# A gated linear recurrence with a GEGLU layer behind it: group order by chunk instead of by batch, and the log-magnitude from summed squares

## The chip, the cores and the metric

The kernel runs on one core of a Trainium2 chip. The metric is the device time in microseconds (us), from the start of the program to its end. Before the change it is 317.31 us, the median of 13 runs (312.91 to 322.17).

## What is computed

Four batches, eight heads, 768 time steps, head dimension 48. The first half is a recurrence with a complex decay for each head and channel, whose real part alone is read out; its output, 3072 tokens of 384 channels, goes through a gated GELU layer with a residual:

```python
mag = sqrt(a_re**2 + a_im**2)
a = (a_re + 1j * a_im) * minimum(mag, 0.999) / (mag + 1e-6)
for t in range(768):                      # per batch and head
    S = a[t, :, None] * S + k[t, :, None] * v[t, None, :]
    y[t] = q[t] @ real(S)
x = y.transpose(0, 2, 1, 3).reshape(3072, 384)
g = x @ w_gate                            # 384 x 1536
h = 0.5 * g * (1 + erf(g / sqrt(2))) * (x @ w_val)
out = x + sigmoid(x @ w_res) * (h @ w_out)
```

## The kernel before

**Recurrence as masked attention.** The product of decays from one step to another is the exponential of a difference of cumulative sums. So the kernel takes the logarithm of each decay (log-magnitude `lm` and phase `th`), sums both along time by matmuls with triangular matrices, and multiplies q by the exponential of the sum (`E`) and its cosine and sine, k by the inverse exponential (`Ei`) and the same cosine and sine. Inside 128 tokens the recurrence then is a masked product of such q and k with v; what lies before is carried as a state of 96x48 per head (`G`, and its bf16 copy `Gb`).

**Groups, units, stages.** A group is one batch and one of its three chunks of 256 tokens, and within it two halves of 128 tokens, so there are 12 groups. In the program they are numbered batch by batch (`b, s = divmod(g, NS)` in `rows`): group 0, 1, 2 are the three chunks of batch 0. The number s of the chunk decides how a group begins: s = 0 with an empty state, s = 1 and 2 with what the chunk before left. Units hold the groups that go through the GELU layer together: [0], [1, 2], [3, 4], [5, 6], [7, 8], [9, 10], [11]. For each unit u there are two stages, which follow one another, X(u) then Y(u):

- X(u), `phase_x` (L550): the log and exp pass of the groups of unit u+2 (`p1_steps`, L189), the cumulative sums of log-magnitude of unit u+1 (`cs_l`, L216) and their exps, then arctans of unit u+2 (`p1_arctan`), the cumulative sums of the phase of unit u+1 (`cs_t`, L246) with the reduction of the angle to a fraction of a turn (two DVE operations per half, then one that clears the sign), the sines and cosines (`p2_sin`, L270), the second half of the attention of unit u, and the output products of unit u-1 (`op_step`, L501). X(-1) and X(0) differ: X(-1) does all of it for group 0 alone, and X(0) does the log pass and the sums for groups 1 and 2 and then the log pass for 3 and 4.
- Y(u), `phase_y` (L599): the gate and value products of unit u with their gelus (`gv_step`, L474: twelve sets of a PSUM tile `gp` and one `vp`, one gelu on ACT, one multiplication on DVE), the residual gate (`rp_step`, L491), the products of q and k with exps and sines of unit u+1 (`products`, L327) and the first half of the attention of unit u+1 (`attention`, L354).

The order inside a stage is written out by hand: `weave` places each list of steps between two fractions of the stage and emits the steps in that order; each engine works off its own queue in that order. Log and exp, arctan and sine, and gelu and tanh each need a table of ACT's; so a stage X has two table loads and a stage Y one (`table`, L517), 21 in all, and a manual dependence keeps every ACT function that needs a table in emitted order.

**The log pass of one group** takes, on 128x768 tiles, four ACT operations and three on DVE:

```python
lm = Ln(ar);  s = Exp(-lm);  th = s * ai;  s = Square(th)
s = Ln(s + 1);  lm = min(0.5 * s + lm, LNMAX)     # arctan(th) comes later
```

**The decay over a chunk border** is needed as a factor per head and channel (`M`) laid out along the partitions. For groups 1, 2 and 4 it comes from matmuls with a vector of ones (`sums`, 48 of them, and `sums_exp`). For later groups with s > 0, three rows (the first log-magnitude, the last `E` of the group before, the first `Ei`) are written to DRAM and read back transposed by POOL's DMA queue (`turn`, L279; `decay0` to `decay3`), and `decay3` multiplies them on DVE at the end of the X stage. For groups from `TURN` = 5 on, q and k are transposed by DMA (`trp`); before, by TensorE.

**Loads.** SP's queue issues, in this order, a of group 0 (real and imaginary part, each in two halves: L143 to L147), q and k of group 0 (L150), a of groups 1 to 4, q and k of 1 and 2, and later groups. POOL's queue holds v (L157), and the weights (L163): `after_landing` (L178) places a tiny POOL copy that reads a loaded tile, and issues the weights behind it; so weights come after a of groups 1 to 4 has landed, w_out after k of group 2. Tiles of a are in pools of six buffers (`lda`), q and k in pools of four (`ldq`); the products go to tiles of their own (`pK`). Outputs are written by SP (`ot`), and x is accumulated onto them in DRAM by POOL's queue (L514).

## Time and profile before

| what | value |
|---|---|
| median of 13 runs | 317.31 us (312.91 to 322.17) |
| the profiled execution, its own time | 316.8 us |
| its span, first to last instruction | 315.0 us |
| granted clock of TensorE, mean | 0.938 of full speed |
| TensorE matmuls (PE) | 261.2 us busy, 83% of the span |
| TensorE weight loads (PEld, beside PE) | 161.0 us, 51% |
| VectorE (DVE) | 226.2 us, 72% |
| ScalarE (ACT) | 194.3 us, 62% |
| GpSimd (POOL) | 81.1 us, 26% |
| DMA | 41.87 MB, mean 133 GB/s |

The stages, from the table load on ACT that begins each to the next stage's:

| stage | from | length, us | PE busy | DVE busy | ACT busy |
|---|---|---|---|---|---|
| loads and X(-1) | 0.00 | 23.50 | 5.86 | 8.12 | 10.22 |
| X(0) | 23.50 | 41.65 | 27.24 | 32.06 | 28.59 |
| Y(0) | 65.15 | 18.99 | 18.14 | 16.30 | 12.09 |
| X(1) | 84.14 | 18.67 | 13.47 | 13.85 | 17.20 |
| Y(1) | 102.81 | 25.47 | 25.05 | 22.36 | 16.69 |
| X(2) | 128.28 | 18.79 | 15.75 | 14.31 | 17.04 |
| Y(2) | 147.07 | 23.81 | 21.71 | 16.74 | 11.53 |

Busy time is the time in which an engine executes; an engine that waits for another's result is not busy. The row with the highest busy time in a stage is the engine that would set the stage's length if nothing else did; where no row comes near the length, the stage is a chain of waits. Line numbers (L134) are those of the kernel before; `act` and its L134 issue all ACT functions, so those are told apart by their tiles.

### The profile page before, as it was taken

To read this page: it belongs to the slowest core of one execution; us is meant where nothing else is said; L and a number is where in the kernel's file an instruction comes from. 1 tells how busy PE (TensorE), PEld (TensorE's weight loads), DVE (VectorE), ACT (ScalarE), POOL (GpSimd) and SP (SyncE) were. 2 spreads that over 40 slices of the span, in tenths; PEclk is the share of its full clock that TensorE was granted. 3 is DMA by queue.
4 is the path that set the end of the run, shared out by engine and by line. 5 is a ranking of instruction groups with operands and counts; after the bars stand their busy time and mean duration, and the time that the engine had idled before them with its cause. 6 is when DMAs were issued, how large, how long until landed. Compare 5 with 4: busy or idle time off the path is not lost.

```text
span 315.0 us, 5372 instructions
## 1 busy us (share of the span) xinstructions
PE 261.2 (83%) x1976; PEld 161.0 (51%) x1976; DVE 226.2 (72%) x404; ACT 194.3 (62%) x325; POOL 81.1 (26%) x119
## 2 busy tenths in 40 slices
PE   0336936879967999789979989999999996999994
PEld 0115633568734566445436654566545663446682
DVE  1346857879569997299944899887997767445452
ACT  4539686276798756997427976559664644355150
POOL 4105641013051502047202374101711031200220
PEclk9995675959999999999979999999999998999999
DMA  7999999999999995079997389930399014910531
GB/s 155 205 192 190 189 161 173 169 193 193 180 186 206 206 189 41 0 138 172 190 221 94 44 149 130 218 66 25 55 183 211 0 28 100 183 27 0 131 71 52
DMA packets 166874, 41.87 MB, mean 133 GB/s; under 512 B 155968, under 2 KB 166848, under 8 KB 166848
## 3 DMA queue, kind: packets, MB, share of 16 engines
q1 hardware_dynamic: 132416, 30.94, 51.2%
q0 software_dynamic: 34432, 10.59, 31.4%
q8 instruction: 15, 0.25, 0.3%
q14 instruction: 11, 0.09, 0.1%
HBM read 31.31 MB, written 9.07 MB: 128 GB/s over the span
## 4 chain that ended last, share of the span: by engine, by line
PE 59%; ACT 14%; DVE 10%; DMA 7%; issue 4%; SPq 4%; POOL 0%; DVEq 0%; ACTq 0%
PE gp L481 14%; PE vp L485 13%; PE op L505 9%; ACT s L134 4%; ACT L519 3%; PE cst L259 3%; PE rp L497 3%; PE csl L222 3%; DMA ar<-in_a_re_dram 3%; ACT ar L134 2%; SPq L146 2%; PE at L372 2%; DMA KT<-padK 2%; PE cst L261 2%; SPq L154 2%
## 5 line engine op out<-in xcount | busy, mean ns | idle before, releaser
L134 ACT ACTIVATE h<-gp 128x512 bf16<-128x512 f32 (+1 forms) x84 | 44.8, 536 | 47.1 <-PE gp L481 46.7
L481 PE MATMUL gp<-xT,wg 128*128 128x512 bf16 (+1 forms) x252 | 63.1, 355 | 2.1 <-DVE xT L472 1.1
L488 DVE SCALAR_TENSOR_TENSOR h<-h,vp 128x512 bf16<-128x512 bf16 (+1 forms) x84 | 50.2, 606 | 20.2 <-PE vp L485 16.5
L485 PE MATMUL vp<-xT,wv 128*128 128x512 bf16 (+1 forms) x252 | 63.3, 354 | 0.0
L505 PE MATMUL op<-wo,h 128*128 128x384 bf16 x288 | 52.5, 333 | 4.9 <-ACT Ei L134 3.0
L505 PEld LDWEIGHTS <-h 128*128 128x128 bf16 x288 | 28.1, 100 | 23.9 <-issue 8.2
L514 POOL DMA_DIRECT2D out_dram<-x x22 | 20.7, 954 | 66.3 <-DMA out_dram<-ot 62.3
L485 PEld LDWEIGHTS <-wv 128*128 128x128 bf16 x252 | 24.7, 100 | 21.2 <-issue 1.2
L481 PEld LDWEIGHTS <-wg 128*128 128x128 bf16 x252 | 23.9, 100 | 18.9 <-issue 2.9
L519 ACT ACT_TABLE_LOAD x21 | 26.9, 1283 | 1.1 <-PEq L657 0.7
L160 POOL DMA_DIRECT2D v<-in_v_dram x24 | 22.1, 924 | 4.5 <-issue 1.9
L375 DVE TENSOR_TENSOR atm<-at,mask 128x512 bf16<-128x512 f32 x28 | 19.2, 685 | 5.4 <-PE at L372 5.4
L199 DVE TENSOR_TENSOR ai<-s,ai 128x768 f32<-128x768 f32 x12 | 11.1, 955 | 16.4 <-ACT s L134 10.8
L259 PE MATMUL cst<-ai,lt0b 128*128 128x384 f32 x24 | 11.9, 579 | 12.9 <-ACT ai L134 11.0
L134 ACT ACTIVATE CS<-ai,hpi 128x768 bf16<-128x768 f32 x11 | 10.3, 933 | 17.9 <-DVE ai L267 17.9
L222 PE MATMUL csl<-ar,lt0a 128*128 128x384 f32 x24 | 11.5, 567 | 11.0 <-DMA ar<-in_a_re_dram 11.0
L508 DVE SCALAR_TENSOR_TENSOR ot<-sg,op 128x384 f32<-128x384 f32 x24 | 13.2, 548 | 9.6 <-PE op L505 8.4
L181 POOL COPY landed<-k 1x1 f32<-1x1 f32 x10 | 3.4, 338 | 63.6 <-DMA k<-in_k_dram 63.6
L438 ACT CAST x<-y 128x384 bf16<-128x384 f32 x24 | 11.5, 478 | 12.5 <-PE y L435 11.3
L286 POOL DMA_DIRECT2D m<-dm x20 | 16.9, 884 | 8.8 <-DMA dm<-Ei 4.5
L398 DVE TENSOR_TENSOR atm<-at,mask 128x512 bf16<-128x512 f32 x20 | 13.7, 686 | 5.1 <-PE at L395 5.0
L134 ACT ACTIVATE sg<-rp 128x384 f32<-128x384 f32 x24 | 11.7, 492 | 8.2 <-PE rp L497 8.2
(98 smaller groups left out, 513.7 us busy)
## 6 DMA issues: line engine op xcount, KB each, us to landing
ar<-in_a_re_dram SPq DMA_DIRECT2D x24, 192.0 KB, 5.0
ai<-in_a_im_dram SPq DMA_DIRECT2D x24, 192.0 KB, 4.7
q<-in_q_dram SPq DMA_DIRECT2D x24, 192.0 KB, 4.0
k<-in_k_dram SPq DMA_DIRECT2D x24, 192.0 KB, 4.0
out_dram<-ot SPq DMA_DIRECT2D x24, 192.0 KB, 2.6
out_dram<-x POOLq DMA_DIRECT2D x22, 192.0 KB, 4.3
v<-in_v_dram POOLq DMA_DIRECT2D x24, 96.0 KB, 5.4
wg<-in_moe_w_gate_dram POOLq DMA_DIRECT2D x4, 288.0 KB, 10.9
```

Source lines behind the costliest of these rows:

```text
L134: tab(nc.scalar.activation(**kw))
L160: nc.gpsimd.dma_start(out=t[:, c], in_=rows(v, g, c))
L222: nc.tensor.matmul(out=cs, lhsT=lmat[c], rhs=T["lm", g][:, sl], start=True, stop=True)
L259: nc.tensor.matmul(out=cs, lhsT=tmat[c], rhs=th[:, sl], start=True, stop=(s == 0))
L286: nc.gpsimd.dma_start(out=m[u * D:(u + 1) * D].rearrange("p r h -> p (r h)"), in_=md.rearrange("r (h d) -> d (r h)", h=H))
L375: nc.vector.tensor_tensor(out=atm, in0=at, in1=mask4, op=OP.mult)
L481: nc.tensor.matmul(out=gp, lhsT=wg[:, fi, ffi * 128:(ffi + 1) * 128], rhs=xT[:, fi, :], start=(fi == 0), stop=(fi == KD - 1))
L485: nc.tensor.matmul(out=vp, lhsT=wv[:, fi, ffi * 128:(ffi + 1) * 128], rhs=xT[:, fi, :], start=(fi == 0), stop=(fi == KD - 1))
L488: nc.vector.scalar_tensor_tensor(out=h2[:, ffi, :], in0=h2[:, ffi, :], scalar=0.5, in1=vp, op0=OP.mult, op1=OP.mult)
L505: nc.tensor.matmul(out=ps, lhsT=h2[:, ffi, jj * 128:(jj + 1) * 128], rhs=wo[:, ffi, :], start=(ffi == 0), stop=(ffi == KF - 1))
L514: nc.gpsimd.dma_start(out=out[t0:t0 + 128, :], in_=T["x", token(u, jj)], accum_op=OP.add)
L519: tab(nc.scalar.preload_act_table_set(nm))
```

## The change

- **Order.** Groups are numbered by chunk: the first chunk of all four batches is groups 0 to 3, the second 4 to 7, the third 8 to 11. What is carried (the phase sum `R`, the state `G`) is kept per batch. Units stay as they are.
- **Log-magnitude.** `lm` is half of Ln(ar*ar + ai*ai). The two Squares and the addition are emitted in Y stages (`squares`), tied behind the last gelu and the last gate multiplication emitted before; the log pass keeps Ln(lm), Ln(ar), Exp(-Ln(ar)), and one DVE operation takes the half and the minimum.
- **First stages.** `ramp` replaces X(-1) and X(0): groups 0, 1 and 2 share one log and exp pass and one pass of arctans and sines; 19 table loads in all. Group 0's attention is written out as a whole (`attention_first`). X(1) does the log pass and the sums of unit [3, 4] together; X(2) those of [5, 6] and the log pass of [7, 8] (`P1AT`); from X(3) on the log pass is again two units ahead.
- **Decays.** All eight groups with s > 0 take the way through DRAM; `sums` and `sums_exp` are gone; the multiplication is placed at 0.55 of Y.
- **Memory and loads.** q and k are multiplied in place; pools change sizes. Loads of weights and of q, k and a of groups 1 to 4 wait for the landing of a named earlier load (`held`); SP issues those of groups 1 to 4 behind three small row copies (`T["row"]`).

```diff
     UNITS = [[0]] + [[g, g + 1] for g in range(1, NG - 1, 2)] + [[NG - 1]]
     NU = len(UNITS)
-    FIRST = UNITS[0][-1]
-    NEAR = UNITS[2][-1]
+    ORD = [(b, s) for s in range(NS) for b in range(B)]
+    assert NS == 3 and B == 4 and len(ORD) == NG
+    CHUNK = [b * NS + s for b, s in ORD]
+    NEXT = {g: ORD.index((b, s + 1)) for g, (b, s) in enumerate(ORD) if s < NS - 1}
+    P1AT = {2: 1, 3: 2, 4: 2}
...
     lda = ctx.enter_context(tc.tile_pool(name="lda", bufs=6))
-    ldq = ctx.enter_context(tc.tile_pool(name="ldq", bufs=4))
+    ldr = ctx.enter_context(tc.tile_pool(name="ldr", bufs=4))
+    pB = ctx.enter_context(tc.tile_pool(name="pB", bufs=1))
+    ldq = ctx.enter_context(tc.tile_pool(name="ldq", bufs=3))
     ldv = ctx.enter_context(tc.tile_pool(name="ldv", bufs=6))
-    pS = ctx.enter_context(tc.tile_pool(name="pS", bufs=2))
+    pS = ctx.enter_context(tc.tile_pool(name="pS", bufs=4))
     pE = ctx.enter_context(tc.tile_pool(name="pE", bufs=2))
...
-    xp = ctx.enter_context(tc.tile_pool(name="xp", bufs=9))
+    xp = ctx.enter_context(tc.tile_pool(name="xp", bufs=8))
...
     def rows(a, g, c):
-        b, s = divmod(g, NS)
+        b, s = ORD[g]
         t0 = (s * C + c) * 128
...
+    def held(i, after):
+
+        if after is not None:
+            tc.add_manual_dep(i.ins, after.ins.name, behind, reason="load order")
+        return i
...
+    def squares(g):
+
+        def q0():
+            T["lm", g] = pS.tile([128, W], FP, tag="s", name="lm")
+            with paced("gelu"):
+                nc.scalar.activation(out=T["lm", g], in_=flat(T["ar", g]), func=AF.Square)
+
+        def q1():
+            t = pB.tile([128, W], FP, tag="sq", name="sq")
+            with paced("gelu"):
+                nc.scalar.activation(out=t, in_=flat(T["ai", g]), func=AF.Square)
+            with paced("gmul"):
+                nc.vector.tensor_tensor(out=T["lm", g], in0=T["lm", g], in1=t, op=OP.add)
+        return [q0, q1]
+
     def p1_steps(g):
 
         def s0():
-            T["lm", g] = flat(T["ar", g])
+            lm = T["lm", g]
+            act(out=lm, in_=lm, func=AF.Ln)
+            nc.vector.tensor_scalar(out=lm, in0=lm, scalar1=0.5, scalar2=LNMAX, op0=OP.mult, op1=OP.min)
+
+        def s1():
+            T["s", g] = flat(T["ar", g])
+            act(out=T["s", g], in_=T["s", g], func=AF.Ln)
+
+        def s2():
             T["th", g] = flat(T["ai", g])
-            act(out=T["lm", g], in_=T["lm", g], func=AF.Ln)
-
-        def s1():
-            T["s", g] = pS.tile([128, W], FP, tag="s", name="s")
-            act(out=T["s", g], in_=T["lm", g], func=AF.Exp, scale=-1.0)
+            act(out=T["s", g], in_=T["s", g], func=AF.Exp, scale=-1.0)
             nc.vector.tensor_tensor(out=T["th", g], in0=T["s", g], in1=T["th", g], op=OP.mult)
-
-        def s2():
-            act(out=T["s", g], in_=T["th", g], func=AF.Square)
-
-        def s3():
-            act(out=T["s", g], in_=T["s", g], func=AF.Ln, bias=1.0)
-            lm = T["lm", g]
-            nc.vector.scalar_tensor_tensor(out=lm, in0=T["s", g], scalar=0.5, in1=lm, op0=OP.mult, op1=OP.add)
-            nc.vector.tensor_scalar(out=lm, in0=lm, scalar1=LNMAX, scalar2=None, op0=OP.min)
-
-        return [s0, s1, s2, s3]
+        return [s0, s1, s2]
...
-            T["R"] = st1.tile([128, DM], FP, tag="R", name="R")
-            nc.vector.tensor_copy(out=T["R"], in_=T["th", g][:, DM:W])
+            T["R", b] = st1.tile([128, DM], FP, tag="R%d" % b, name="R")
+            nc.vector.tensor_copy(out=T["R", b], in_=T["th", g][:, DM:W])
         elif s < NS - 1:
-            nc.vector.tensor_tensor(out=T["R"], in0=T["R"], in1=T["th", g][:, DM:W], op=OP.add)
+            nc.vector.tensor_tensor(out=T["R", b], in0=T["R", b], in1=T["th", g][:, DM:W], op=OP.add)
...
     def decay0(g):
-        turn("m1", g, [T["lm", g][0:1, 0:DM]])
-
-    def decay1(g):
...
     def decay2(g):
-        turn("m2", g, [T["E", g - 1][127:128, DM:W], T["Ei", g][0:1, 0:DM]])
+        if g in NEXT.values():
+            nc.gpsimd.dma_start(out=T["md", g][1:2, :], in_=T["Ei", g][0:1, 0:DM])
+            turn("m2", g, T["md", g], 2)
+        if g in NEXT:
+            md = dr.tile([2, DM], FP, tag="d2", name="d2")
+            T["row"] = (nc.sync if ORD[g][1] == 0 else nc.gpsimd).dma_start(out=md[0:1, :], in_=T["E", g][127:128, DM:W])
+            T["md", NEXT[g]] = md
 
     def decay3(g):
+        if g not in NEXT.values():
+            return
+        with paced("gmul"):
+            multiply(g)
+
+    def multiply(g):
         m = T["m2", g]
         M = mp.tile([128, H], FP, tag="M", name="M")
...
-    def sums(g):
...
     def products(g):
         def x0():
-            qE = pK.tile([128, W], BF, tag="qE", name="qE")
+            qE = flat(T["q", g]).bitcast(BF)[:, 0:W]
             nc.vector.tensor_tensor(out=qE, in0=flat(T["q", g]), in1=T["E", g], op=OP.mult)
             T["qE", g] = qE
 
         def x1():
-            kE = pK.tile([128, W], BF, tag="kE", name="kE")
+            kE = flat(T["k", g]).bitcast(BF)[:, 0:W]
             nc.vector.tensor_tensor(out=kE, in0=flat(T["k", g]), in1=T["Ei", g], op=OP.mult)
             T["kE", g] = kE
 
@@ -349,8 +366,43 @@
...
+    def enter_state(g):
+
+        b, s = ORD[g]
+        if s == 0:
+            return
+        G = T["G", b]
+        Mb = T["M", g][0:DD].rearrange("p (h u) -> p h u", u=1).to_broadcast([DD, H, D])
+        nc.vector.tensor_tensor(out=G[0:DD], in0=G[0:DD], in1=Mb, op=OP.mult)
+        Gb = stt.tile([128, H, D], BF, tag="Gb", name="Gb")
+        nc.vector.tensor_copy(out=Gb[0:DD], in_=G[0:DD])
+        T["Gbf"] = Gb
+
...
+    def leave_state(g):
+
+        b, s = ORD[g]
+        if s == NS - 1:
+            return
+        d = T["dk", g][0:DD].rearrange("p (h d) -> p h d", h=H)
+        if s == 0:
+            T["G", b] = st1.tile([128, H, D], FP, tag="G%d" % b, name="G")
+            nc.vector.tensor_copy(out=T["G", b][0:DD], in_=d)
+        else:
+            nc.vector.tensor_tensor(out=T["G", b][0:DD], in0=d, in1=T["G", b][0:DD], op=OP.add)
...
+    def attention_first(g, u, j0):
...
+        return [call(tr, 0), call(tr, 1), call(dk, 0), call(tr, 2), call(sc, 0), call(tr, 3), call(sc, 1), call(yy, 0),
+                call(sc, 2), call(sc, 3), call(dk, 1), call(xt_step, u, j0), call(yy, 1), call(xt_step, u, j0 + 1)]
...
                              start=(fi == 0), stop=(fi == KD - 1))
-        act(out=h2[:, ffi, :], in_=gp, func=AF.Gelu)
-        nc.vector.scalar_tensor_tensor(out=h2[:, ffi, :], in0=h2[:, ffi, :], scalar=0.5, in1=vp,
...
-        t0 = token(u, jj) * 128
+        t0 = (CHUNK[UNITS[u][0] + jj // C] * C + jj % C) * 128
...
-        g1, g2 = gs(u + 1), gs(u + 2)
-        d1 = [g for g in g1 if g % NS > 0 and g > NEAR]
+        g1 = gs(u + 1)
+        p1g = [g for w in range(NU) if P1AT.get(w, w - 2) == u for g in gs(w)]
+        now = [g for g in p1g if g in g1]
+        ahead = [g for g in p1g if g not in g1]
         ops = [call(op_step, u - 1, jj) for jj in range(len(gs(u - 1)) * C)]
...
         def p1(g):
-            return p1_steps(g) + ([call(decay0, g)] if g % NS > 0 and g > NEAR else [])
+            return p1_steps(g) + [call(decay0, g)]
...
-        dec = [call(decay2, g) for g in d1]
-        atn = [table("trig_and_small")] + [call(p1_arctan, g) for g in g2]
+        dec = [call(decay2, g) for g in g1]
...
-        dec3 = [call(decay3, g) for g in d1]
...
+        if now:
+            atn = [table("trig_and_small")] + [call(p1_arctan, g) for g in now + ahead]
+            pn = zip_steps([p1(g) for g in now])
+            weave((0.0, 0.05, pn[:2]), (0.06, 0.1, csls), (0.12, 0.25, pn[2:]), (0.26, 0.4, exs),
+                  (0.28, 0.48, zip_steps([p1(g) for g in ahead])),
+                  (0.5, 0.5, dec), (0.55, 0.65, atn), (0.62, 0.8, cst), (0.9, 0.95, sin),
+                  (0.0, 0.8, att), (0.0, 0.25, ops) if u == 1 else (0.1, 1.0, ops))
+            return
+        atn = [table("trig_and_small")] + [call(p1_arctan, g) for g in ahead]
+        weave((0.0, 0.12, csls), (0.05, 0.5, zip_steps([p1(g) for g in ahead])), (0.12, 0.45, exs),
+              (0.46, 0.46, dec), (0.2, 0.65, cst), (0.7, 0.95, atn + sin), (0.0, 0.8, att), (0.1, 1.0, ops))
...
+    def ramp():
+
+        g0, g1, g2 = gs(0) + gs(1)
...
+        def cst(g):
+            for c in range(C):
+                cs_t(g, c)
+        p = {g: p1_steps(g) for g in (g0, g1, g2)}
+        q = {g: squares(g) for g in (g0, g1, g2)}
+        table("natural_log_exp_and_others")()
+        for f in q[g0] + p[g0][:2] + q[g1] + p[g1][:1]:
+            f()
+        csl(g0)
+        for f in p[g0][2:] + q[g2]:
+            f()
+        ex(g0)
+        csl(g1)
+        for f in p[g2][:1] + p[g1][1:]:
+            f()
+        ex(g1)
+        csl(g2)
+        for f in p[g2][1:]:
+            f()
+        ex(g2)
+        with tc.issue_after(T["row"].ins):
+            load_q(1, T["ld", "w", 0])
+            load_q(2, T["ld", "w", 2])
+            for g in gs(2):
+                load_a(g, T["ld", "w", 3])
+        table("trig_and_small")()
+        pr = products(g0)
+        pr[0]()
+        pr[2]()
+        for g in (g0, g1, g2):
+            p1_arctan(g)
+            cst(g)
+        p2_sin(g0)
+        pr[1]()
+        pr[3]()
+        p2_sin(g1)
+        last = T["abs"]
+        a0 = attention_first(g0, 0, 0)
+        for f in a0[:5]:
+            f()
+        p2_sin(g2)
+        for f in a0[5:]:
+            f()
+        T["last"] = last
...
+        def late(f):
+            with tc.issue_after(T["last"].ins):
+                f()
+        dec3 = [call(decay3, g) for g in gs(u + 1)]
+        sq = [f for w in range(NU) if P1AT.get(w, w - 2) == u + 1 for g in gs(w) for f in squares(g)]
         pr = [st for g in gs(u + 1) for st in products(g)]
-        weave((0.0, 1.0, gv), (0.0, 0.4, pr), (0.3, 0.95, att_steps(u + 1, 0)) if u < 2 else (LATE0, LATE1, att_steps(u + 1, 0)))
...
+        if u == 0:
+            pr = [call(late, f) for f in pr]
+        weave((0.0, 1.0, gv), (0.0, 0.4, pr), (0.55, 0.56, dec3), (0.5, 0.95, sq), (0.3, 0.95, att_steps(u + 1, 0)) if u < 2 else (LATE0, LATE1, att_steps(u + 1, 0)))
...
+    for g in range(3):
         load_a(g)
...
+    load_q(0)
+    load_v(0, T["ld", "ai", 1])
+    for i in range(4):
+        load_w_in(i, T["ld", "ai", 1])
+    load_v(1, T["ld", "w", 0])
+    load_w_res()
+    load_v(2, T["ld", "w", 1])
+    load_w_out()
+    ramp()
+    for u in range(NU + 1):
+        if u > 0:
+            phase_x(u)
+        while T["a"] < min(NG, gs(u + 1)[-1] + 6 if gs(u + 1) else NG):
...
         phase_y(u)
-        for g in gs(u + 3):
+        for g in gs(u + 2 if u == 0 else u + 3) + (gs(3) if u == 0 else []):
             load_q(g)
             after_landing(T["k", g], call(load_v, g))
```

## What I predicted before it ran

> **What bounds the kernel now.** I read the page's slices first, then busy time by stage (the loads of the Activation tables mark the stages), then the timelines and the chain of waits inside the stages that the change touches. The slices are the busy tenths of each engine, the granted clock of TensorE and the share of the DMA engines:
>
> ```profile
> PE   0336936879967999789979989999999996999994
> ...
> ACT  4539686276798756997427976559664644355150
> ...
> PEclk9995675959999999999979999999999998999999
> DMA  7999999999999995079997389930399014910531
> ```
>
> From slice 8 on (63 us) PE is full; before it is not, and its clock drops to half. The DMA engines are full until slice 15. By stage (columns: us, then busy us of PE, PEld, DVE, ACT, POOL, granted clock, DMA share, GB/s):
>
> ```profile
> 23.50:65.15 41.65, 27.24 (x202) 20.22 (x203) 32.06 (x53) 28.59 (x44) 14.20 (x18) 0.70 1.31 177
> 65.15:84.14 18.99, 18.14 (x229) 15.53 (x229) 16.30 (x37) 12.09 (x26) 4.33 (x6) 0.84 1.29 187
> 84.14:102.81 18.67, 13.47 (x70) 7.23 (x69) 13.85 (x25) 17.20 (x27) 5.66 (x10) 1.00 1.30 196
> 102.81:128.28 25.47, 25.05 (x268) 16.24 (x266) 22.36 (x40) 16.69 (x31) 6.25 (x10) 1.00 0.90 133
> 128.28:147.07 18.79, 15.75 (x79) 8.74 (x78) 14.31 (x28) 17.04 (x26) 8.02 (x13) 1.00 0.54 94
> ```
>
> These are X(0), Y(0), X(1), Y(1), X(2). The Y stages are PE's, the X stages from X(1) are ACT's (17.20 of 18.67, 17.04 of 18.79), and X(0) is a serial chain that no engine fills. Its end on ACT, with the idle time before a row and its releaser in brackets:
>
> ```profile
> 48.09 1.28 ACT L519 ACT_TABLE_LOAD   x1
> 49.39 3.04 ACT L134 ACTIVATE ai<-ai 128x768 f32<-128x768 f32 x4
> 57.56 0.94 ACT L134 ACTIVATE CS<-ai,hpi 128x768 bf16<-128x768 f32 x1 [5.13 <-DVE ai L267]
> ...
> 62.98 0.94 ACT L134 ACTIVATE CS<-ai,hpi 128x768 bf16<-128x768 f32 x1 [3.75 <-DVE ai L267]
> ...
> 65.15 1.28 ACT L519 ACT_TABLE_LOAD   x1
> ```
>
> Four arctans, 5.13 us of waiting for DVE's fractions, sines, waiting again: the first gelu (66.45) comes 18.4 us after that table load began. Such a chain is what a stage costs whose arctans are not done beforehand.
>
> **The ramp.** The new program has one log/exp pass and one trig pass for three groups, 19 table loads instead of 21. ACT's start to the next start is 1.30 us per load (48.09 to 49.39), so two loads are 2.6 us, inside the ramp. The Trainium skill ("ScalarE: Activation LUTs", What ACT_TABLE_LOAD costs) adds a drain of about 1.38 us to each load; by it the two would be an estimated 5.3 us, but these rows leave no room for a drain.
>
> I laid the new order on each engine out by hand with durations of this trace: 0.84 us for a 128x768 activation (about 0.75 back to back), 0.39 for a 128x384 exp, 0.95 and 0.55 for DVE's 128x768 product and scalar operation, 0.55 for 128x384 (0.47 back to back), 1.45 to 1.65 for a cold fp32 cumulative matmul pair. Loads: the first operand is used at 4.49 and the sixth tile has landed at 14.27, so 1.95 us per tile. The real and imaginary parts of groups 0, 1, 2 are then there at 4.4, 6.5, 8.6, 10.3, 12.2 and, shared with v, about 16. ACT works without a gap from there: Square, exp, two Ln, Exp, four exps, Ln, Exp, four exps, 9.0 us, to 25.2; trig load to 26.5; three arctans to 29.0 (the third waits for DVE, which has waited in its queue for k of group 0, estimated at 26.3). Then DVE: R copies, twelve operations of 128x384, three of 128x768 and padQ, padK of group 0: 15 at 0.55 and 2 at 0.95, 10.1 us, to 39.1. The products of group 1 take 1.8 (40.9), group 0's copies and masks 4.6 (45.5), the last y, cast, transpose and first gp 3.2: first gelu at 48.7 against 66.45, **17.75 us earlier**. PE does not enter this: its cumulative sums end by 34.
>
> What feeds it: q and k of group 1 are now issued by SP only behind three small copies, the last of which waits for the exps at 25.2, and weights run on POOL's queue meanwhile. What a half tile takes from issue to landing (last column, us) beside other loads alone, and beside weights:
>
> ```profile
> k<-in_k_dram SPq DMA_DIRECT2D x2, 192.0 KB, 4.6
> ```
>
> ```profile
> wg<-in_moe_w_gate_dram POOLq DMA_DIRECT2D x4, 288.0 KB, 10.9
> ...
> k<-in_k_dram SPq DMA_DIRECT2D x3, 192.0 KB, 11.7
> ```
>
> The first answer is for issues at 24 to 28 us, the second for 28 to 36. The last half of k of group 1 is issued at about 28, so it lands between 32.6 and 39.7; I take 38, as it runs beside weights. DVE asks for it at about 39.9. That is 2 us of cover; whatever k is later than that, all of DVE's queue behind it (every copy and mask of group 0's attention) is later too.
>
> **Y(0).** Before, X(0) had already run five gate/value sets and the first transposes and key sums of group 1 (PE rows at 57.5 to 65); now Y(0) has them all, about 4 us of PE, while two products and two adds more make DVE 20 us long. From first gelu to the next table load 17.7 becomes 22: **+4.3**. Its four Squares (3.4 us) lie in ACT's 6.9 us of idle time.
>
> **X(1).** Groups 3 and 4 now do logs, exps, arctans, sums and sines in one stage. ACT to the trig load: table 1.3, six activations 4.5, a cast and a small copy 0.7, eight exps 3.0: 9.5 us. Then, after X(0)'s pattern with two groups: load and two arctans 2.8, up to the first fractions 4.0 to 6, sines 1.7, second fractions 1.5 to 3, sines 1.7, in all 12 to 15: 21.5 to 24.7 against 18.67. I take 22.2, nearer the warm end because PE has work until the arctans: **+3.5**.
>
> **Y(1)** gains eight Squares (6.7 us on ACT, 16.69 of 25.47 busy) and four adds (3.5 on DVE, whose products of group 4 leave). Hidden if perfectly spread; if each delays a gelu by 0.25 to 0.5, 2 to 4 us. I take **+2**.
>
> **X(2)** has four groups of logs. ACT: table 1.3, twelve activations 8.8, eight exps 3.0, four small copies 1.5, a copy 0.4, table 1.3, four arctans 3.0: 19.2. DVE's R updates of all four groups stand ahead of the first fraction in its queue; from there 3.4 us if PE is warm, 5 if cold, sines 1.7, second fractions 1.9, sines 1.7: 28 to 30 against 18.79. I take 28.8: **+10**. Nothing hides it: PE has 17 us of work there.
>
> Whether PE is cold after such a gap, this shows (PE's timeline in X(5), where POOL's m transfer kept DVE waiting 2.12 us and so ACT and PE):
>
> ```profile
> 262.80 0.18 PE L435 MATMUL y<-Gb,QT 96*128 96x48 bf16 x1
> 265.77 0.47 PE L466 MATMUL tpx<-ident,x 128*128 128x128 bf16 x3 [2.79 <-ACT x L438]
> 266.03 3.71 PE L505 MATMUL op<-wo,h 128*128 128x384 bf16 x12
> ```
>
> Twelve op matmuls are 1.95 us elsewhere. So 2.8 us of idleness sufficed here. The skill ("TensorE: Matmul & The Clock Gate", Part 1) asks for an idle window of about 3.4 us; by it X(1)'s gap of some 3 us could stay warm and the sum be 1 us lower, while X(2)'s gap of 4 us is cold by both. That rule speaks against longer X stages.
>
> **Given back later.** decay3 moves into the Y stages, so X(5)'s wait goes: 2.1 us and half of the 1.76 us of cold op matmuls, perhaps all and a gap left over: 2 to 4.5, I take **-3.3**; next is DVE's chain to the sines. In Y(2) PE waited 2.1 us for KT landing behind a loads (the chain's "DMA KT<-padK" at 154.36); X(2) is longer and those loads are issued earlier in it, so 0 to 3, **-2.5**. X(3) and X(4) lose an activation per group (0.75 each, PE-bound, so little) and get two more carry matmul pairs in X(4), 1.3: **+0.8**. The 48 ms matmuls (4.4 us of PE) lay in the ramp and are in its sum. Decay rows for all eight groups are small transfers on POOL's queue, ahead of the x accumulations, whose readers come a stage later: 0, and 1 to 2 where v of a group stands behind one.
>
> **Sum.** -17.75 +4.3 +3.5 +2 +10 -2.5 +0.8 -3.3 = -2.95. Span 315.0 becomes 312.05; with the 1.8 us around it the profiled 316.8 becomes 313.85. The median of the 13 runs, 317.31, is 0.5 above that execution; I say 314.
>
> **The rivals.** (B) The moved logs cost less: X(2) +6, X(1) +1.5, Y(1) 0, because casts and exps fill ACT's waits: 8 us less, 306. For it: ACT idles 5.13 and 3.75 in X(0)'s chain. Against: DVE's queue fixes that order, and it holds little else. (C) Slower: the loads set the ramp. Queued halves beside weights land about 5 us apart at worst (two k halves issued from 30.12 stretched over 5.76 us of issue); four of them from 28 end at 48, 8 us after DVE wants k of group 1, and 8 us on the first gelu: 322. It decides once k lands after 39.9. For it: the DMA row at 9 throughout. Against: weights are mostly down by then. (D) The ramp's gain comes back as hunger in X(1): q and k of groups 3 and 4 land, by adding up transfers at full rate, at about 77, X(1) asks for them from 75 to 79; 3 us late and the time is about unchanged, 317. That the change does not do what it says can be left out: the built program has 24 Squares and 19 loads.
>
> **How the numbers follow.** Forecast 0.50 (309 to 317 from its terms), B 0.18, C 0.20, D 0.12. About 0.5% (1.6 us) is what a measurement of this kernel can tell. Faster: B and 0.74 of the forecast, 0.55. Slower: C, 0.4 of D and a tenth of the forecast, 0.30. The rest 0.15. The range takes B and C in: 305 to 322.
>
> **What would show it.** Right: gelu's first load near 43 and first gelu near 49; X(1) about 22 and X(2) about 29 us long with ACT nearly full; no DVE wait for m. Wrong: DVE idle on in_k or in_q at 39 to 48 (C) or in X(1) (D); X(2) under 26 (B); Y(1) above 28.

## The result: slower, and the profile after

The changed kernel takes 322.32 us (median of 11 runs, 318.10 to 325.37) where the kernel before takes 318.17 (48 runs); the ratio is 1.019, interval 1.015 to 1.023. (Ratios compare the fast executions alone and leave out those that fell into a second, slower state, so they are not the quotients of the medians.) I had said 314, with 305 to 322 as the range and 0.30 for slower. Its profiled execution took 319.5 us, span 317.7: one of its faster ones. The slices of its page:

```profile
PE   0455478995879994839799999889999998999994
...
ACT  3795384788556799972657986548664573446150
...
PEclk9985767999599998968799999999999999999998
DMA  7999999999997992476999548997369304920541
```

PE fills earlier than before, but has new holes in slices 9, 15 and 17 (counted from 0, 7.9 us each), with the clock down to 0.5 in slice 10 and 0.6 in 17, and the DMA engines are nearly full to slice 15. The stages from X(1) to Y(3) (columns as before):

```profile
70.11:94.60 24.49, 17.95 (x95) 9.96 (x94) 17.89 (x32) 16.79 (x26) 7.76 (x12) 0.86 1.42 177
94.60:120.50 25.90, 23.52 (x246) 14.72 (x245) 23.06 (x42) 21.04 (x38) 8.15 (x12) 1.00 1.13 149
120.50:152.80 32.30, 23.59 (x98) 12.77 (x98) 21.92 (x36) 23.27 (x36) 13.65 (x21) 0.84 0.54 93
152.80:174.57 21.77, 19.97 (x144) 10.29 (x143) 16.62 (x30) 14.08 (x25) 4.34 (x6) 0.92 1.19 189
174.57:193.63 19.06, 18.19 (x137) 11.42 (x137) 17.60 (x31) 16.93 (x27) 11.22 (x16) 1.00 0.44 50
193.63:217.56 23.93, 21.39 (x166) 11.44 (x164) 18.91 (x35) 12.98 (x23) 5.44 (x8) 1.00 1.27 198
```

X(1) starts at 70.11 instead of 84.14, 14 us earlier. But by then ACT has 44.8 us of work behind it, where it had 50.9 at the same point before: six logs and exps and two arctans of groups 3 and 4 are still to come. (PE has 43.3 us of matmuls behind it instead of 51.2, but 4.4 us of that difference are the 48 `ms` matmuls, which the change does away with.) X(1) and X(2) take 56.8 us instead of 37.5, and in X(2) no engine is busy for more than 23.6 of 32.3 us. So 19.3 us come back in two stages, more than the first stages gained.

### The profile page after: what moved, and what is told of

Read it like the earlier page. It is cut to its first block, busy times and chain, and to the rows that moved or that the text cites. A ratio compares the mean times of both kernels' runs of the same rounds, so it can differ in the third digit from the quotient of the medians.

```text
span 317.7 us, 5322 instructions
## 1 busy us (share of the span) xinstructions
PE 261.6 (82%) x1928; PEld 157.0 (49%) x1928; DVE 227.2 (72%) x408; ACT 201.1 (63%) x335; POOL 88.7 (28%) x133
## 3 DMA queue, kind: packets, MB, share of 16 engines
q0 software_dynamic: 34976, 10.63, 32.3%
## 4 chain that ended last, share of the span: by engine, by line
PE 49%; DVE 16%; DMA 13%; ACT 12%; SPq 6%; issue 4%; DVEq 0%; ACTq 0%
PE gp L573 11%; PE op L597 11%; PE vp L577 10%; DMA k<-in_k_dram 8%; PE cst L286 4%; SPq L159 3%; PE cst L288 3%; DMA KT<-padK 3%; SPq L167 2%; ACT L611 2%; PE rp L589 2%; DVE lm L290 2%; DVE lm L291 2%; PE at L424 2%; DVE ai L236 2%
## 5 line engine op out<-in xcount | busy, mean ns | idle before, releaser
L139 ACT ACTIVATE h<-gp 128x512 bf16<-128x512 f32 (+1 forms) x84 | 44.8, 537 | 44.8 <-PE gp L573 42.7
L597 PE MATMUL op<-wo,h 128*128 128x384 bf16 x288 | 51.5, 329 | 4.3 <-ACT Ei L139 4.3
L577 PEld LDWEIGHTS <-wv 128*128 128x128 bf16 x252 | 24.6, 99 | 21.5 <-issue 1.5
L573 PEld LDWEIGHTS <-wg 128*128 128x128 bf16 x252 | 23.9, 99 | 19.2 <-issue 3.8
L254 PE MATMUL csl<-lm,lt0a 128*128 128x384 f32 x24 | 13.0, 632 | 20.7 <-DVE lm L227 20.7
L309 POOL DMA_DIRECT2D m<-d x32 | 22.8, 718 | 22.0 <-DVE M L341 8.8
L196 POOL COPY landed<-k 1x1 f32<-1x1 f32 x9 | 1.6, 182 | 92.6 <-DMA k<-in_k_dram 92.6
L139 ACT ACTIVATE CS<-ai,hpi 128x768 bf16<-128x768 f32 x12 | 11.2, 934 | 22.9 <-DVE ai L294 22.9
L173 POOL DMA_DIRECT2D v<-in_v_dram x24 | 21.6, 907 | 13.7 <-DMA ai<-in_a_im_dram 7.8
L286 PE MATMUL cst<-ai,lt0b 128*128 128x384 f32 x24 | 13.8, 665 | 11.6 <-ACT ai L139 9.7
L427 DVE TENSOR_TENSOR atm<-at,mask 128x512 bf16<-128x512 f32 x28 | 19.1, 683 | 4.5 <-PE at L424 4.5
L219 DVE TENSOR_TENSOR lm<-lm,sq 128x768 f32<-128x768 f32 x12 | 11.4, 951 | 11.2 <-ACT sq L217 11.1
L139 ACT ACTIVATE ar<-ar 128x768 f32<-128x768 f32 x24 | 19.3, 839 | 0.1
L479 ACT CAST x<-y 128x384 bf16<-128x384 f32 x22 | 10.5, 478 | 12.1 <-PE y L476 12.0
L254 PEld LDWEIGHTS csl<-lm,lt0a 128*128 128x128 f32 x24 | 4.6, 222 | 24.7 <-DVE lm L227 23.5
## 6 DMA issues: line engine op xcount, KB each, us to landing
wg<-in_moe_w_gate_dram POOLq DMA_DIRECT2D x4, 288.0 KB, 10.8
```

The source lines that it names most:

```text
L139: return tab(nc.scalar.activation(**kw))
L173: held(nc.gpsimd.dma_start(out=t[:, c], in_=rows(v, g, c)), after)
L254: nc.tensor.matmul(out=cs, lhsT=lmat[c], rhs=T["lm", g][:, sl], start=True, stop=True)
L286: nc.tensor.matmul(out=cs, lhsT=tmat[c], rhs=th[:, sl], start=True, stop=(s == 0))
L309: nc.gpsimd.dma_start(out=m[u * D:(u + 1) * D].rearrange("p r h -> p (r h)"), in_=md.rearrange("r (h d) -> d (r h)", h=H))
L427: nc.vector.tensor_tensor(out=atm, in0=at, in1=mask4, op=OP.mult)
```

## The experiments

Stage lengths are from each run's own profile, medians and ratios from the runs beside it on the same chip; line numbers in a profile line are those of the kernel that it shows. "The changed kernel" has the stages above; where another of its profiles is meant, it is called "again". By their times alone k1, wolate and warm cannot be told from the changed kernel (ratios 1.016 and 1.019): for these the traces count.

**again.** No edit.

> The changed kernel once more, unaltered, beside the others on the same chip. If its profiled execution of 319.5 us was a lucky one (the median of its runs is 322.3, and the kernels with the same first stages and the same Y(3) show 1.5 and 1 us more there), this profile shows a span near 320.5, with the first gelu at 52 to 53 and Y(3) at 24 to 25 us. If the 2.8 us between that profile and the median lie elsewhere, those stages are as in the first profile and another is longer.

320.89 us, ratio 1.016 (1.010 to 1.022); this profile's span is 322.3. First gelu 53.73, Y(0) 25.03, Y(1) 27.39, Y(3) 24.61, so each of these is 0.7 to 2.2 us longer than in the first profile; X(1) is 1.0 shorter, X(2) nearly the same (32.56). The two executions differ in the stages that the loads feed, more of them than I had named. With 319.5 us the first was among the fastest of its kernel; with 324.06 us this one is the slowest of its seven, so the usual execution lies between the two.

### The loads

Why the first gelu came at 51.5 instead of 48.7 is seen in DVE's timeline of the changed kernel, and in its chain of waits (start, us, what):

```profile
21.52 0.95 DVE L236 TENSOR_TENSOR ai<-ar,ai 128x768 f32<-128x768 f32 x1
30.57 0.96 DVE L352 TENSOR_TENSOR k<-k,E 128x768 bf16<-128x768 f32 x1 [8.10 <-DMA k<-in_k_dram]
```

```profile
15.53 14.95 DMA k<-in_k_dram
```

The second half of k of group 0, issued at 15.53 together with the first weights, takes 15 us; DVE waits 8.1 us for it, with the phase work of three groups behind it in its queue. Rival C named this mechanism for k of group 1; it struck one group earlier.

**k0.** Weights behind k of group 0:

```diff
-        load_w_in(i, T["ld", "ai", 1])
+        load_w_in(i, T["ld", "k", 0])
```

> The weights wait for the landing of k of group 0 instead of the imaginary part of group 1. Theory F: DVE's wait of 8.1 us for k of group 0 goes (it lands near 19 instead of 30.5), the first gelu comes at about 48 instead of 51.5, limited by k of group 1, which lands at 42 to 44; the whole is 3 us faster. Theory S: the first gelu may come earlier, but the loads of groups 3 and 4 come no earlier, so X(1) takes back what is won and the whole moves by less than 1 us.

325.14 us, ratio 1.036 (1.022 to 1.051). The wait of 8.1 us is gone, and DVE now waits 0.8 and 4.6 us for q and k of group 1; first gelu 53.8, no earlier than in again (53.73):

```profile
45.31 0.96 DVE L352 TENSOR_TENSOR k<-k,Ei 128x768 bf16<-128x768 f32 x1 [4.60 <-DMA k<-in_k_dram]
```

Theory F had named k of group 1 as the next limit, but at 42 to 44 us and with the first gelu at 48. The wait was only handed on.

**k1.** As k0, and q and k of group 1 ahead of the weights:

```diff
     load_q(0)
+    load_q(1)
...
-        load_w_in(i, T["ld", "ai", 1])
+        load_w_in(i, T["ld", "k", 1])
...
-            load_q(1, T["ld", "w", 0])
```

> q and k of group 1 are issued right behind q and k of group 0, and the weights wait for k of group 1: all loads in the order in which they are used. Theory F: k of groups 0 and 1 are there at about 20 and 25, no DVE wait is left in the first 45 us, the first gelu comes at 44 to 46 and the whole is 6 us faster than the changed kernel. Rival: the weights, some 12 us of transfers, then land last, at about 40 to 45, and the first gelu stays at 48 or later; or X(1) takes it back as under S.

321.48 us, ratio 1.022 (1.010 to 1.034). First gelu at 47.81, but X(1) begins at 71.57. ACT's timeline of this run in Y(0):

```profile
59.35 0.84 ACT L212 ACTIVATE lm<-ar 128x768 f32<-128x768 f32 x1 [1.34 <-DMA ar<-in_a_re_dram]
...
61.48 0.84 ACT L217 ACTIVATE sq<-ai 128x768 f32<-128x768 f32 x1 [1.28 <-DMA ai<-in_a_im_dram]
```

The Squares of groups 3 and 4 wait for their operands, and the gelus behind them in ACT's queue wait too. A Square placed among the gelus makes ACT, which PE's results wait for, wait for a late load.

**wolate.** As k1, and w_out behind a of group 4:

```diff
...
-                 T["ld", "w", 3])
+                 after)
...
+        load_w_out(T["ld", "ai", gs(2)[-1]])
```

> As k1 (q and k of group 1 issued right behind those of group 0, weights behind them), and w_out, 12 us of transfers that nobody reads before X(1), waits for the landing of a of group 4. Theory F (Y(0) waits for a of groups 3 and 4, whose Squares stand in ACT's queue ahead of gelus): these land at about 55 instead of 62 to 65, ACT's waits of 1.3 and 1.3 us for them go, X(1) begins at 65 to 67 instead of 71.6 (k1) or 70.1 (the changed kernel), and the whole is 4 to 5 us faster than k1. Rival: Y(0) is DVE's (22 us of work in it), so it ends at 70 whatever lands when, or w_out is late for X(1); then no gain over k1.

321.70 us, ratio 1.022 (1.009 to 1.035). X(1) begins at 67.9, near the 65 to 67 expected, but then lasts 28.7 us. PE's timeline there:

```profile
68.95 0.81 PE L597 MATMUL op<-wo,h 128*128 128x384 bf16 x4 [0.49 <-DMA wo<-in_moe_w_out_dram]
...
72.74 1.33 PE L597 MATMUL op<-wo,h 128*128 128x384 bf16 x4 [2.97 <-DMA wo<-in_moe_w_out_dram]
```

Now w_out is late, since it shares the engines with a of groups 5 and 6, which nobody needs yet.

**need.** As wolate, q and k of groups 3 and 4 behind w_out, a of 5 and later behind those:

```diff
...
+        if u == 0:
+            for g in gs(2):
+                load_q(g, T["ld", "wo"])
+                after_landing(T["k", g], call(load_v, g))
+        with (tc.issue_after(T["ld", "k", gs(2)[-1]].ins) if u == 0 else nullcontext()):
             while T["a"] < min(NG, gs(u + 1)[-1] + 6 if gs(u + 1) else NG):
```

> As wolate, and q and k of groups 3 and 4 wait for the landing of w_out and go ahead of a of groups 5 and 6, which then load alone: every load up to X(1) in the order of its use, and none beside one that is needed earlier. Theory F (the loads, at some 190 GB/s, are what the early start runs into): w_out is down before X(1) begins at 68, q and k of group 4 by 80, X(1) falls from 28.7 (wolate) to 24 us and the whole is 4 us faster than wolate, 317. Rival: nothing more can be won by order because the bytes up to X(1) fill the queues to 80 us anyway; then the wait moves to q and k, or to a of groups 5 and 6 in Y(1), and the time stays at 320 to 322.

316.59 us, ratio 1.004 (1.000 to 1.007): first gelu 48.2, X(1) from 67.3, 24.7 us long. So the order of the loads cost the changed kernel some 4 us (320.89 of its own runs beside these), and only the whole order gave it back; each single step moved the wait to the next load. Even so it is no faster than before.

### The X stages

**p1at.** The logs of groups 5 and 6 in X(1):

```diff
-    P1AT = {2: 1, 3: 2, 4: 2}
+    P1AT = {2: 1, 3: 1, 4: 2}
```

> The log pass of groups 5 and 6 goes from X(2) into X(1) (and their Squares into Y(0)); nothing else changes. Theory S (the X stages that must do logs, sums, arctans and sines of the same groups one after another are what makes the change slow): X(2) falls from 32.3 us to 20 or 21, since its cumulative sums can start at once; X(1) grows by six activations, two decay rows and two arctans, 6.5 us, from 24.5 to 31; Y(0) grows by about 2. In all 3 us faster than the changed kernel. Theory F (the loads set it): the real and imaginary parts of groups 5 and 6 are down only at 65 to 69 us, X(1) starves on them, grows by 10 or more, and nothing is gained.

324.69 us, ratio 1.034 (1.021 to 1.047). X(1) 31.6 and X(2) 18.1, as theory S said: a stage whose logs are done beforehand is 14 us shorter, and the sum of the two falls by 7. But Y(0) grows by 3.5 (by 2.2 against again), and Y(2) and Y(3) by 3.6 and 2.5, where PE now waits 6.2 us in all for KT (2.5 in the changed kernel). It gives no gain.

**warm.** Two output products in X(2) put late:

```diff
...
-                  (0.0, 0.8, att), (0.0, 0.25, ops) if u == 1 else (0.1, 1.0, ops))
+                  (0.0, 0.8, att), (0.0, 0.25, ops) if u == 1 else (0.1, 0.55, ops[:2]),
+                  (0.52, 0.54, [] if u == 1 else [call(op_step, u - 1, 2, "exp"), call(op_step, u - 1, 3, "first row")]))
```

> In X(2) the third and fourth output product wait for the last exponential and for the last decay row, so that PE has work until just before the phase sums; nothing else changes. If TensorE's lowered clock after 4.9 us of idleness is what makes the chain of X(2) long, the first four phase sums take 0.65 to 0.73 us instead of 1.29 to 1.65, the chain from the arctans to the last sines falls from 10.8 to about 7.6 us, X(2) from 32.3 to 29, and the whole is 3 us faster. Rival: DVE and ACT set that chain, and it moves by less than 1 us.

321.58 us, ratio 1.021 (1.005 to 1.036). PE in X(2), first of the changed kernel, then of this one:

```profile
139.87 1.65 PE L286 MATMUL cst<-ai,lt0b 128*128 128x384 f32 x2 [4.92 <-ACT ai L139]
141.31 1.49 PE L288 MATMUL cst<-R,ones2pi 128*128 128x384 f32 x2
142.59 1.49 PE L286 MATMUL cst<-ai,ut0b 128*128 128x384 f32 x2
```

```profile
142.44 0.86 PE L286 MATMUL cst<-ai,lt0b 128*128 128x384 f32 x2
143.14 0.81 PE L288 MATMUL cst<-R,ones2pi 128*128 128x384 f32 x2
143.78 0.81 PE L286 MATMUL cst<-ai,ut0b 128*128 128x384 f32 x2
```

The sums run at full clock, half the time each, but X(2) is only 1.4 us shorter (30.9), since the held products themselves ran until 142.4, some 2 us into the arctans (table load at 139.20), and Y(2) gives 1.0 back. From the first of the eight pairs of sums to the end of the last it is 5.6 us instead of 8.1, so in this chain the lowered clock is worth some 2.5 of the 13.5 us by which X(2) grew: a part of its length, not the main cause.

**needwarm.** need and warm.

> need and warm together: if the two are independent, 1.5 us faster than need (X(2) 31 instead of 32.5), so 315 to 316 under Theory F, the first version of the changed kernel that is faster than before; if X(2)'s gain again comes back as a longer Y(2) and Y(3), no faster than need.

315.98 us, ratio 0.998 (0.993 to 1.003). X(2) 29.95. No difference from before can be told; that it beats need is not shown either.

### One part at a time

**late34.** The kernel before, with logs and arctans of groups 3 and 4 in X(1):

```diff
...
 # X(0)
-                  (0.4, 0.64, zip_steps([p1(g) for g in g2])), (0.641, 0.642, dec3), (0.645, 0.65, atn[:1]),
-                  (0.65, 0.66, [call(p1_arctan, g) for g in g1]), (0.67, 0.85, cst), (0.75, 0.8, atn[1:]),
+                  (0.641, 0.642, dec3), (0.645, 0.65, atn[:1]),
+                  (0.65, 0.66, [call(p1_arctan, g) for g in g1]), (0.67, 0.85, cst),
...
 # X(1)
+            weave((0.0, 0.05, pn[:4]), (0.06, 0.2, pn[4:]), (0.21, 0.24, csls), (0.245, 0.25, sm), (0.26, 0.4, exs),
+                  (0.28, 0.48, zip_steps([p1(g) for g in g2])), (0.5, 0.5, dec3), (0.55, 0.65, atn), (0.62, 0.8, cst),
+                  (0.9, 0.95, sin), (0.0, 0.8, att), (0.0, 0.25, ops))
```

> The kernel before with one thing of the change: the log pass and the arctans of groups 3 and 4 go from X(0), where nothing waits for them, to X(1), which then does logs, sums, arctans and sines of 3 and 4 and the log pass of 5 and 6. Theory W (the early start is borrowed: work that X(0) did beside its own waits is done later in the open): X(0) gets shorter by 4 to 7 us (eight activations of 0.84, of which some lay in waits), X(1) grows from 18.7 to 30 to 32, as X(2) of the changed kernel, and the whole is 6 to 9 us slower than before. Rival: X(0)'s end moves up by as much as X(1) grows, since its chain waits for that pass; then the time is within 2 us of before, and the loss of the changed kernel is the loads' alone.

329.32 us, ratio 1.038 (1.032 to 1.045). Its stages X(0), Y(0), X(1):

```profile
23.54:60.16 36.62, 27.41 (x186) 19.69 (x187) 26.41 (x45) 21.17 (x34) 13.32 (x18) 0.69 1.32 173
60.16:78.57 18.41, 17.49 (x236) 14.80 (x236) 15.66 (x35) 12.03 (x27) 3.85 (x6) 0.88 1.31 184
78.57:113.52 34.95, 19.15 (x96) 11.18 (x94) 23.13 (x36) 25.67 (x38) 9.39 (x13) 0.76 1.16 176
```

ACT has 7.5 us less to do in X(0), which gets 5.1 us shorter; X(1) gets 16.3 us longer. This is theory W, with a larger loss than expected: in X(0) the pass lay partly in waits, in X(1) a second chain of log, sum, exp, arctan, sum and sine stands ahead of everything, and PE's clock falls to 0.76. Loads have no part in it: in X(1) neither PE, ACT nor DVE waits for one. The size is that of the old log form, whose sums wait for the whole pass, and not the price in the changed kernel.

**bord.** The changed kernel, groups batch by batch:

```diff
-    ORD = [(b, s) for s in range(NS) for b in range(B)]
+    ORD = [(b, s) for b in range(B) for s in range(NS)]
```

(with carries and decay rows in the ramp, and the multiplication at 0.2 of Y(0))

> The changed kernel with the groups in the old order, batch by batch; the first stages, log form and loads as changed (groups 1 and 2 now need a carry, two decay rows and a state in the first stages and Y(0)). Theory: the chunk order is what lets three groups share the first passes; without it the ramp gets four more matmul pairs at a lowered clock, 6 us, and Y(0) a chain of states, so X(1) starts 5 us later and the whole is 4 to 6 us slower than the changed kernel. Rival: PE and DVE have room for the carries there, and X(1) and X(2) need fewer; within 2 us of the changed kernel.

330.52 us, ratio 1.051 (1.029 to 1.073); trig load at 34.1 instead of 25.7, X(1) from 80.2 instead of 70.1. This is 8 to 10 us slower than the changed kernel, more than I had expected, but it is not the price of the order alone. Of the 8.4 us at the trig load, 6.6 are a load again. In the old order a row of group 2 needs an exponential ahead of that table load, and this waits for DVE's product, which stands behind k of group 0 in DVE's queue (used at 31.67):

```profile
33.53 0.52 ACT L139 ACTIVATE ar<-lm 1x384 f32<-1x384 f32 x1 [6.63 <-DVE ai L236]
```

What the chunk order is worth with k there in time is not shown.

**oldlog.** The changed kernel with the old log pass for groups 3 to 11:

```diff
+        if g > 2:
+            return p1_old(g)
...
-            weave((0.0, 0.05, pn[:2]), (0.06, 0.1, csls), (0.12, 0.25, pn[2:]), (0.26, 0.4, exs),
+            weave((0.0, 0.2, pn), (0.21, 0.25, csls), (0.26, 0.4, exs),
...
-        sq = [f for w in range(NU) if P1AT.get(w, w - 2) == u + 1 for g in gs(w) for f in squares(g)]
+        sq = [f for w in range(NU) if P1AT.get(w, w - 2) == u + 1 for g in gs(w) if g < 3 for f in squares(g)]
```

> Only the log-magnitude is undone for groups 3 to 11: Ln, Exp, Square, Ln as before, one activation more in X per group, and no Squares or additions in the Y stages; groups 0 to 2 keep the new form. Theory S1 (the new form pays): X(1) grows by 2 and X(2) by 4 us and the Y stages shrink by less than 2 in all, so about 4 us slower than the changed kernel. Theory S2 (the Squares cost more in Y than they save in X): Y(0) and Y(1) shrink by 2 us each, X(2) grows by less than 2; 2 us faster.

338.73 us, ratio 1.079 (1.065 to 1.092): X(1) 29.5, X(2) 38.6, Y(2) 26.7. The direction is S1's, the size four times it. Two more things differ. In the old form the log-magnitude is the last result of the pass, so the cumulative sums come behind all of it: the first `E` starts 11.5 us into X(1) instead of 7.8. And in this kernel the log-magnitude lies in the loads' tiles again, four of them, so loads come later too. How much of the 16 us is which I did not separate.

**blog.** The kernel before with the new log form for groups 5 to 11:

```diff
+        if g <= NEAR:
+            return p1_old(g)
...
+        sq = [f for g in gs(u + 3) if g > NEAR for f in squares(g)]
+        weave((0.0, 1.0, gv), (0.0, 0.4, pr), (0.5, 0.95, sq), (0.3, 0.95, att_steps(u + 1, 0)) if u < 2 else (LATE0, LATE1, att_steps(u + 1, 0)))
```

> The kernel before with the log-magnitude part alone: groups 5 to 11 take Ln of summed squares, Squares and additions in Y(0) to Y(3); order, first stages and loads as before (q and k are multiplied in place, the pool of x holds 8, to make room). Theory S1 (the new form pays by itself): X(1) and X(2), which are ACT's (17.2 of 18.7 and 17.0 of 18.8 us), lose two activations each, 1.5 us, X(3) some 0.5, and the Y stages gain less than 1 in all: 2 to 3 us faster than before. Rival: the Squares delay gelus in Y(0) and Y(1) by as much as X wins, no difference or up to 2 us slower.

318.82 us, ratio 1.010 (0.990 to 1.031), no difference. X(1) and X(2) are 2.8 and 1.8 us shorter, X(3) 6.2 longer. DVE there:

```profile
182.64 0.16 DVE L343 TENSOR_TENSOR M<-m 96x8 f32<-96x8 f32 x1 [1.68 <-DMA m<-dm]
188.67 0.16 DVE L343 TENSOR_TENSOR M<-m 96x8 f32<-96x8 f32 x1 [5.86 <-DMA m<-dm]
```

The stage got shorter than the way of the decay rows through POOL's queue, and the product that waits for them holds up all of DVE.

**blog2.** blog, with the decay product at 0.55 of Y, as the change has it:

```diff
-        dec3 = [call(decay3, g) for g in d1]
+        dec3 = []
...
+        dec3 = [call(paced_decay3, g) for g in gs(u + 1) if g % NS > 0 and g > NEAR]
+        weave((0.0, 1.0, gv), (0.0, 0.4, pr), (0.55, 0.56, dec3), (0.5, 0.95, sq), (0.3, 0.95, att_steps(u + 1, 0)) if u < 2 else (LATE0, LATE1, att_steps(u + 1, 0)))
```

> blog (the kernel before with the log-magnitude part alone), and the decay multiplications at 0.55 of the Y stages, as in the changed kernel. In blog X(1) and X(2) were 2.8 and 1.8 us shorter than before, but X(3) 6.2 us longer: DVE waited 1.7 and 5.9 us for the decay rows, with the phase sums of group 8 in its queue behind. If the new log form pays once nothing waits for the rows, X(3) falls from 27.5 to 19 or 20 and the whole is 310 to 312, 2% faster than before. Rival: the wait goes on into Y(3), whose attention needs the same product, and the time stays near 317.

307.24 us, ratio 0.974 (0.969 to 0.980), some 8 us under the kernel before: X(3) 19.6, X(5) 13.7. This beats both kernels: parts of the change on the order and the first stages of before. By stage, X(1), X(2) and X(3) are 2.6, 1.8 and 1.7 us shorter, X(0) and Y(0) 3.4 longer in all. But the largest single gain is Y(2), 20.3 instead of 23.8, and it is not ACT's: before, PE waits there,

```profile
159.99 0.60 PE L372 MATMUL at<-QT,KT 96*128 96x128 bf16 x4 [2.07 <-DMA KT<-padK]
```

and in blog2 it does not. blog and blog2 also multiply q and k in place and have other pools for the loads; no run separates this from the log form.

**decy.** The kernel before with the decay product in Y alone (the edit of blog2).

> The kernel before with the decay multiplications at 0.55 of the Y stages, as in the changed kernel, and nothing else. The prediction's step: X(5)'s wait of 2.1 us and the cold products behind it go, 2 to 4.5 us, so 3 us faster than before. If that step is right, some 3 of the 9 us that blog2 wins are the placement of this product and 6 are the log form; rival: the wait turns up in Y(5), and blog2's gain is the log form's alone.

314.54 us, ratio 0.995 (0.991 to 1.000). X(5) is 13.7 instead of 15.8 and Y(5) 22.0 instead of 22.9: 3.0 us, the prediction's step, and blog2 has the same 3.0 there. By the ratio the whole is only some 1.5 us shorter. So of blog2's 8 us, 1.5 to 3 are this placement; the rest comes with the log form and the changes of memory that it brings, taken together.

## Right and wrong, step by step

| term, us | said | first profile | again | need |
|---|---|---|---|---|
| first gelu | -17.75 | -14.9 | -12.7 | -18.3 |
| Y(0) from there | +4.3 | +0.9 | +1.7 | +1.5 |
| X(1) | +3.5 | +5.8 | +4.9 | +6.0 |
| Y(1) | +2 | +0.4 | +1.9 | +0.5 |
| X(2) | +10 | +13.5 | +13.8 | +13.7 |
| Y(2) | -2.5 | -2.0 | -2.1 | -2.0 |
| X(3), X(4) | +0.8 | -1.0 | -1.0 | -1.1 |
| Y(3), Y(4) | 0 | +3.7 | +4.4 | +4.3 |
| X(5) to the end | -3.3 | -3.7 | -3.6 | -3.6 |
| sum | -2.95 | +2.7 | +7.3 | +1.1 |

Three steps failed: the landing of k of group 0, the size of X(1) and X(2), and the stall in Y(2), which I took off without a term for where it goes. The column of need tells them apart: with the loads in order of use the first gelu is where I had said, and the kernel is still no faster than before, because of the other two. They would have cost more if Y(0), Y(1), X(3) and X(4) had not been too dear by 6.2 us.

- **The ramp**: ACT's side was right (trig load said 25.2, measured 25.69, and 1.29 us from that load to the next start). The step that failed is the estimate that k of group 0 lands at 26.3; it landed at 30.5, and near 32 in again. The price of a half tile beside weights, 11.7 us, stood in my own row, and I applied it to k of group 1 only. That step is C's mechanism, but DVE was idle for it from 22.5 to 30.6, not from 39 to 48, where I had said to look. Taking this one wait away gained nothing (k0); the order of all loads is shown by need to cost about 4 us. That the time comes out at C's 322 is chance: C had 8 us on the first gelu, it was 2.8 and 5.0, and the rest lies in X(1), X(2) and Y(3).
- **X(1) and X(2)**, the two terms that decided the sign: the mechanism was right, the size was off by 2.3 and 3.5 us (2.5 and 3.7 in need). ACT was not nearly full in X(2), as I had said for the right case: 23.3 of 32.3 us. In X(2) I had ACT at the end of the arctans after 19.2 us; it was 21.5, of which 1.5 us are four waits of the small row exponentials for DVE's product, which I had counted as work without a wait:

```profile
126.59 0.52 ACT L139 ACTIVATE ar<-lm 1x384 f32<-1x384 f32 x1 [0.29 <-DVE ai L236]
127.46 0.52 ACT L139 ACTIVATE ar<-lm 1x384 f32<-1x384 f32 x1 [0.34 <-DVE ai L236]
...
136.27 0.52 ACT L139 ACTIVATE ar<-lm 1x384 f32<-1x384 f32 x1 [0.57 <-DVE ai L236]
137.14 0.52 ACT L139 ACTIVATE ar<-lm 1x384 f32<-1x384 f32 x1 [0.34 <-DVE ai L236]
...
147.65 0.94 ACT L139 ACTIVATE CS<-ai,hpi 128x768 bf16<-128x768 f32 x1 [5.63 <-DVE ai L294]
```

  From there to the next table I had 9.6, and it was 10.8. The same row wait is 1.16 us in X(1), where the trig load came after 10.8 us and I had said 9.5. B, by which these logs would cost less, was the wrong side to look on.
- **Y(2) to Y(3)**: the wait for KT did leave Y(2), but PE has it in Y(3):

```profile
207.88 0.40 PE L424 MATMUL at<-QT,KT 96*128 96x128 bf16 x4 [2.46 <-DMA KT<-padK]
```

  It was 2.07 in Y(2) before. I booked the stall as gone without asking what is late next. (1.3 us of Y(3)'s growth is PE work that X(3) lost.)
- **X(5)** and the decay move were right, and decy shows them alone in its stages. **Y(0) and Y(1)** I had too dear (Y(1) not in again, where it is +1.9); the Squares do fit between gelus where their operands are there.
- **D**, hunger for q and k of groups 3 and 4: 0.69 us of DVE's time in the first profile and none in again, so not this.
- **The clock rule.** I weighed an idle window of about 3.4 us (the Trainium skill, "TensorE: Matmul & The Clock Gate", Part 1) against the row of 2.79. In X(1) of the changed kernel PE idles 3.02 us and the twelve products behind it take 2.86 us where a row of twelve at full clock is 2.11 (the 1.95 that I had set beside 3.71 is the time to the next start): the row decides. But the length of the gap does not decide alone: in warm 2.56 us of idleness were followed by a lowered clock (24 products in 5.51 us instead of 4.06), in needwarm 2.57 us were not (12 in 2.12).

## What to carry to other kernels

An earlier start of a stage is not a gain until the work left undone at that point has been subtracted: here X(1) began 14.0 us earlier, and it and X(2) then took 19.3 us longer. Work that lies partly in the waits of a start-up chain costs less than its length, and the same work in a stage that must do a whole dependent chain can cost far more (late34: 7.5 us of ACT, 5.1 us won in X(0), 16.3 lost in X(1)). When loads fill the queues, as here, reordering one only moves the wait to the next; lay out all of them by first use, or leave them. And take a change apart: its small part, with the memory changes that came with it, was worth 8 us, and the whole of it lost 5 to 6.

## What I had not expected of the hardware

A half tile of 192 KB took 15 us when issued beside eight weight transfers (k's median over the run is 4.5); and two executions of one program differ by 2.2 us at the first gelu, at the waits for such loads (8.1 and 8.2 us in front of the same DVE product, 1.6 and 3.3 in front of the one before it).
